# Retuning an instruction planner: longer v runs, a moved constant load, and a new order around the first expert's gather

## The chip, the cores and the metric

The kernel runs on one core of a Trainium2 chip. The core has five engines with an instruction queue of their own: PE (TensorE: matrix products and transposes), DVE (VectorE), ACT (ScalarE), POOL (GpSimd) and SP (SyncE, which here only issues DMA transfers). Each engine takes its instructions strictly in the order in which the program lists them, and semaphores make it wait for data of another engine or of a transfer. The metric is the device time of one execution in microseconds (us); less is better.

## The reference

Three stages follow each other. The first is attention with a mask by hash bucket: a query sees only the keys whose six hash bits are its own.

```python
q_bits = (np.einsum('bhsd,dk->bhsk', q, proj) > 0).astype(np.int64)   # B=2, H=8, S=768, D=64, 6 bits
k_bits = (np.einsum('bhsd,dk->bhsk', k, proj) > 0).astype(np.int64)
mask = q_bucket[:, :, :, None] == k_bucket[:, :, None, :]
scores = np.where(mask, scale * np.matmul(q, k.transpose(0, 1, 3, 2)), -1000000000.0)
attn = softmax(scores)
x = np.matmul(attn, v)                       # becomes 1536 tokens x 512
h = np.maximum(x @ w_in, 0.0)                # 512 -> 2048
x = (h * h @ w_out)                          # 2048 -> 512
```

The third is a layer of eight experts with 192 places each. All (token, expert) pairs are taken in falling order of their logit; a token goes to the first expert that still has a place.

```python
logits = x @ w_gate                          # 1536 x 8
for idx in np.argsort(-logits.flatten()):
    tok, e = (int(idx) // E, int(idx) % E)
    if assigned[tok] >= 0 or counts[e] >= 192:
        continue
    assigned[tok] = e
    counts[e] += 1
for e in range(8):
    out[assigned == e] = np.maximum(x[assigned == e] @ w1[e], 0.0) @ w2[e]   # 512 -> 1024 -> 512
```

## The kernel before, in words

**Planner.** The kernel does not issue instructions as its code is written. Each piece is given to a planner (`Sched`, `S.add`) with an engine, a planned duration, the pieces that it depends on, a priority and the buffers that it takes and gives back. The planner makes one list for each engine. The tables `PR`, `MP`, `EP`, `RP`, `FP` and the numbers `PREP`, `PREP1` and `DL` are priorities and planned costs; changing them changes the order of the lists and nothing that is computed. A dependency in the planner places a piece in its list. Only a use of the same data makes a semaphore in the program.

**Attention.** Eight pairs of heads are worked on, in 96 units of 128 queries by 768 keys. Per unit: four score products on PE (L578), the maximum on DVE (L594), the exponential on ACT (L597), the normalisation on POOL (L606), transposes on PE (L614), a split into two float parts on ACT and DVE (L622, L626), and two products with v on PE (L635, L636). Scores and mask are one product: under the 64 rows of q and k stand 64 rows of a one-hot code of the bucket.

**Preparation of the next pair.** It runs among the units of the pair before. SP loads q, k and v (L449, 384 KB each). PE transposes q and k (L453), ACT and DVE split them (L456, L462, L464), PE takes the bit products (L486) and the one-hot products (L492), ACT writes the one-hot codes (L497, L499) and splits v (L504, with L508 on POOL). SP copies the parts to the rows of the score operand within the on-chip memory (L259).

**Router and experts.** After the two dense layers, the router gathers logits and ranks; the comparisons on DVE (L1357) compare each token's values with all others, and PE counts the comparisons by products with ones (L1364, twelve for a comparison). The indices of the first expert's tokens come out at L1487 (`ix`); POOL then gathers these tokens' rows in two indirect transfers (L1662), PE transposes them (L1680, L1682), DVE and ACT copy the result (L1689, L1687), and the first expert product starts (L1718). The routing of the second expert needs the counts: it begins with L1400. Where PE would be idle here, it runs products on constants whose results nobody reads (`keep`, L1094). POOL's slot casts follow the routing.

Of the kernel before, what the change touches and what calls it, by code (L numbers as in the profile page):

```python
# [7 lines left out]
F32 = mybir.dt.float32  # L8
R = mybir.dt.float32r
# [225 lines left out]
PREP, PW, DL = -21, 0.8, 3.5  # L235
PREP1 = 3
LDP = (2, 0)
PR = {"S": 10.5, "mx": 907, "ex": 577.5, "dn": -268.5, "rec": -506.5, "nrm": 32, "tp": 16, "hi": -161, "lo": -447.5, "pv": 16, "oa": 45.5, "od": 261, "pe": -93, "pa": -360, "pd": -559.5}
# [14 lines left out]
def attention(nc, S, ps, mem, ident, q, k, v, proj, pat, xhi, xlo):  # L253
# [185 lines left out]
    def pair(pr, cm):  # L439
# [61 lines left out]
        def v_act(h):  # L501
            if h == 0:
                T["V", pr] = mem(S.unit(T["vi", pr], "V"), [6, 2, 2, 64], R)
            nc.scalar.activation(T["V", pr][:, :, h, h], T["raw", pr, "v"][:, :, h], AF.Copy)  # L504

        def v_pool(h):
            V = T["V", pr]
            nc.gpsimd.tensor_tensor(V[:, :, h, 1 - h], T["raw", pr, "v"][:, :, h], V[:, :, h, h].bitcast(F32), op=OP.subtract)  # L508
# [207 lines left out]
MP = {"ac": -331, "h1": 412, "h2": 438.5, "ch": -270, "cv": -245, "sp": -195.5, "lg": -262, "ev": -350, "lv": 292, "c0": 4704.5, "c1": 6115, "b0": 487.5, "b1": 3914}  # L716


def mlp(nc, S, ps, mem, ident, xhi, xlo, w_in, w_out, w_gate, wgt, x2d, L, att):
# [285 lines left out]
    return [ld[n] for n in range(12)], st, [i for f in range(16) for i in Wd[f]], []  # L1005


EP = {"fr": -157.5, "lr": -611, "row": 283.5, "col": -247, "cp": 1168.5, "ca": 992.5, "gp": 518}
# [7 lines left out]
RP = {"fr": 355, "se": -191, "oh": 241.5, "G": 263, "A": 634, "lr": -371, "pf": 48, "id": -515.5, "gp": 334, "sq": -73, "G1": 273.5, "A1": 207, "ei": -374, "up": -78}  # L1016
ACT_TILES = {12: (10, 11), 9: (8,), 6: ()}
KEEP = 60
# [18 lines left out]
class Router:  # L1037
# [9 lines left out]
    def __init__(self, tc, ctx, mem, ident, rc):  # L1047
# [5 lines left out]
        nc.sync.dma_start(k, rc)  # L1053
# [914 lines left out]
```

## Time and profile before

| what | us |
|---|---|
| time, median of three runs (lowest, highest) | 778.84 (776.38, 780.49) |
| the profiled execution: time | 779.57 |
| the profiled execution: span of its instructions | 777.8 |
| PE busy in the span | 756.5 (97%) |
| DVE, ACT, POOL busy | 528.3, 420.0, 388.0 |
| mean granted clock of PE, as a share of full speed | 0.987 |

The span goes from the first to the last instruction of the execution; the time has 1.77 us more around it. By the lines that run in it, attention takes the first 258 us, the two dense layers the time to 545, the early router that to 560, the routing of the first expert that to 575, and the experts the rest. An engine is busy while one of its instructions runs; waiting in its queue is not counted.

### The profile page before, as it was taken

Reading aid. Unit: us, or ns where it says so; the run is one execution under the profiler, and the core shown is the slowest. Engines: PE = TensorE matmul, PEld = TensorE weight load, DVE = VectorE, ACT = ScalarE, POOL = GpSimd, SP = SyncE. Lnnn points to the kernel's source line nnn. Section 1 sums busy time; section 2 is a strip of 40 time slices with the busy share of each in tenths; the row PEclk is TensorE's granted clock in tenths of the full one; section 3 lists DMA queues with packets and bytes.
Section 4 is the critical chain, followed back from the end, with each engine's and each line's share of the span. In section 5 each row is a group of like instructions: output and inputs, shape, how many; then the busy total and the mean of one; then the engine's idle time right before and its main releaser. Section 6 shows DMA issues by size and latency. Waiting matters only on the chain.

```text
span 777.8 us, 13945 instructions
## 1 busy us (share of the span) xinstructions
PE 756.5 (97%) x5018; PEld 667.5 (86%) x5018; DVE 528.3 (68%) x1118; ACT 420.0 (54%) x837; POOL 388.0 (50%) x397
## 2 busy tenths in 40 slices
PE   8989999999998999999999999999999999999996
PEld 6767988988887899899899899898679998888885
DVE  6879989999999876822861772245877768763342
ACT  7878999999998764622432343243432322333332
POOL 3667878778888785642562463226421220242111
PEclk9999999999999999999999999999789999999999
DMA  7967576585531133310330110011266366789200
GB/s 174 240 147 165 124 160 142 126 174 136 127 85 56 62 104 106 109 54 1 109 109 2 54 55 1 7 75 54 79 206 220 112 239 221 258 286 342 91 20 21
DMA packets 87973, 94.34 MB, mean 121 GB/s; under 512 B 41920, under 2 KB 66880, under 8 KB 87904
## 3 DMA queue, kind: packets, MB, share of 16 engines
q1 hardware_dynamic: 85856, 87.16, 39.5%
q0 software_dynamic: 2048, 6.29, 2.5%
q8 instruction: 40, 0.66, 0.3%
q14 instruction: 29, 0.24, 0.1%
HBM read 63.55 MB, written 6.29 MB: 90 GB/s over the span
## 4 chain that ended last, share of the span: by engine, by line
PE 72%; issue 9%; DVE 6%; DMA 4%; ACT 4%; POOL 3%; SPq 2%; ACTq 0%; POOLq 0%; DVEq 0%
PE psS L829 11%; PE psTP L802 9%; PE psm L802 9%; PE psS L1718 7%; PE psS L578 5%; PE psS L1759 3%; PE psTP L829 3%; PE psTP L614 3%; PE psO L829 3%; SPq L259 2%; DVE p L626 2%; DMA f<-in_v_dram 2%; DMA r<-r 1%; DVE f L594 1%; PE psTP L1364 1%
## 5 line engine op out<-in xcount | busy, mean ns | idle before, releaser
L606 POOL TENSOR_TENSOR f<-f 128x768 f32<-128x768 f32 x96 | 140.6, 1467 | 28.8 <-PE psTP L614 8.8
L815 POOL TENSOR_TENSOR r<-f,r 128x384 fp32r<-128x384 f32 x64 | 86.5, 1357 | 90.5 <-ACT r L813 77.9
L829 PE MATMUL psS<-r 128*128 128x512 f32 x384 | 95.9, 395 | 0.0
L594 DVE TENSOR_REDUCE f<-psS 128x1 f32<-128x768 f32 x96 | 90.9, 948 | 6.5 <-PE psS L578 6.3
L578 PE MATMUL psS<-r 128*128 128x384 f32 x384 | 88.0, 350 | 2.0 <-ACT f L597 1.1
L597 ACT ACTIVATE f<-psS,f 128x768 f32<-128x768 f32 x96 | 87.2, 909 | 4.3 <-DVE f L594 1.4
L829 PEld LDWEIGHTS psS<-r 128*128 128x128 f32 x384 | 70.8, 188 | 13.1
L811 DVE TENSOR_TENSOR f<-f,psTP 128x384 f32<-128x384 f32 x32 | 17.7, 553 | 88.6 <-ACT f L809 88.3
L1718 PE MATMUL psS<-ff,rf 128*128 128x192 f32 x400 | 76.5, 332 | 0.0
L802 PE MATMUL psTP<-r 128*128 128x384 f32 x384 | 73.4, 338 | 0.7 <-POOL r L792 0.7
L802 PE MATMUL psm<-r 128*128 128x384 f32 x384 | 71.8, 334 | 0.0
L578 PEld LDWEIGHTS psS<-r 128*128 128x128 f32 x384 | 65.2, 188 | 6.6 <-ACT f L597 4.8
L802 PEld LDWEIGHTS psTP<-r 128*128 128x128 f32 x384 | 67.9, 188 | 3.1 <-POOL r L792 1.0
L802 PEld LDWEIGHTS psm<-r 128*128 128x128 f32 x384 | 67.1, 188 | 0.1
L1718 PEld LDWEIGHTS psS<-ff,rf 128*128 128x128 f32 x400 | 64.6, 190 | 1.1
L1662 POOL DMA_INDIRECT ff<-x2d,ix x16 | 19.2, 1200 | 88.0 <-DVE ix L1487 53.5
L1841 POOL DMA_INDIRECT out_dram<-ff,ix x16 | 16.7, 1047 | 92.0 <-DVE ff L1852 67.5
L626 DVE TENSOR_TENSOR p<-psTP,p 128x384 fp32r<-128x384 f32 x102 | 54.8, 547 | 5.0 <-ACT p L622 4.5
L813 ACT ACTIVATE r<-f 128x384 fp32r<-128x384 f32 x64 | 33.5, 523 | 39.3 <-DVE f L811 39.3
L792 POOL TENSOR_TENSOR r<-f,r 128x1024 fp32r<-128x1024 f32 x16 | 40.4, 2525 | 28.5 <-ACT r L790 28.2
L622 ACT ACTIVATE p<-psTP 128x384 fp32r<-128x384 f32 x102 | 49.7, 502 | 6.7 <-PE psTP L614 5.5
L809 ACT ACTIVATE f<-psTP 128x384 f32<-128x384 f32 x32 | 15.6, 489 | 64.5 <-PE psTP L802 63.2
(398 smaller groups left out, 1745.4 us busy)
## 6 DMA issues: line engine op xcount, KB each, us to landing
rf<-in_moe_w_dram SPq DMA_DIRECT2D x60, 512.0 KB, 6.2
r<-r SPq DMA_DIRECT2D x90, 192.0 KB, 4.1
f<-in_moe_w_in_dram SPq DMA_DIRECT2D x16, 512.0 KB, 3.7
f<-in_moe_w_out_dram SPq DMA_DIRECT2D x16, 512.0 KB, 4.6
r<-r SPq DMA_DIRECT2D x15, 384.0 KB, 3.8
f<-in_q_dram SPq DMA_DIRECT2D x8, 384.0 KB, 5.2
f<-in_k_dram SPq DMA_DIRECT2D x8, 384.0 KB, 5.8
f<-in_v_dram SPq DMA_DIRECT2D x8, 384.0 KB, 4.7
```

Of the source, the lines that this page charges most:

```text
L578: nc.tensor.matmul(sbank(u)[:, hf, 0:384], T["q", (pr, h)][:, n, 128 * i:128 * i + 128], T["k", (pr, h)][:, n, 384 * hf:384 * hf + 384], s ...
L594: nc.vector.tensor_reduce(col(0, u), sbank(u)[:, :, 0:384], axis=AX.XY, op=OP.max, negate=True)
L597: nc.scalar.activation(P(u).rearrange("p (a b) -> p a b", a=2), sbank(u)[:, :, 0:384], AF.Exp, bias=col(0, u), accum_out=col(1, u))
L606: nc.gpsimd.tensor_tensor(Pn(u), P(u), col(3, u).to_broadcast([128, 768]), op=OP.mult)
L622: nc.scalar.activation(th, tp(u, g), AF.Copy)
L626: nc.vector.tensor_tensor(tl, tp(u, g), th.bitcast(F32), op=OP.subtract)
L792: nc.gpsimd.tensor_tensor(lo, F, hi.bitcast(F32), op=OP.subtract)
L802: nc.tensor.matmul(hbank(s, hf), w[:, c], y[:, x, sl], start=(c == 0 and i == 0), stop=(c == 3 and i == 2))
L813: nc.scalar.activation(hh[:, sl], r, AF.Copy)
L815: nc.gpsimd.tensor_tensor(hl[:, sl], r, hh[:, sl].bitcast(F32), op=OP.subtract)
L829: nc.tensor.matmul(abank(i), a[:, t], w, start=(f == RUNS[r][1][0] and j == 0), stop=(f == RUNS[r][1][-1] and j == 2))
L1718: nc.tensor.matmul(abank(n)[:, j], raw(p, g)[:, 0, 256 * c + 128 * j:256 * c + 128 * j + 128], xT(p)[:, c], start=(c == 0), stop=(c == 3))
```

## The change

It has four parts.

1. The load of v puts the two heads of a pair one after the other in a partition, so that a partition's piece of a head is one run of 1536 bytes in both memories instead of six of 256. The split of v (L504, L508) reads the new layout.
2. Planned costs of the transfers and of the first gather, and all priority tables, are replaced. This moves instructions on every engine.
3. The load of the router's constants (`rck`, L1053 in the kernel before, the first transfer on SP) is handed to the planner, which puts it eighth.
4. In the second phase of the first routing, the comparisons on DVE from the third on get a planner dependency on the first gather, and POOL's slot casts one on the last early comparison. The idle-time products of `keep` write a spare bank of the tile `z` (two of its banks belong to it, one was unused) instead of taking a bank from the pool; they may be placed from the end of the dense layers on, and 90 of them are allowed instead of 60.

```diff
-PREP, PW, DL = -21, 0.8, 3.5
-PREP1 = 3
+PREP, PW, DL = 56.5, 0.8, 2.4
+PREP1 = -29.5
...
-            a = T["raw", pr, nm] = mem(S.unit(T["li", pr, nm], "raw" + nm), [6, 2, 64])
-            nc.sync.dma_start(a, {"q": q, "k": k, "v": v}[nm][b, hh:hh + 2].rearrange("h (p j) d -> p j h d", p=128))
+            x = {"q": q, "k": k, "v": v}[nm][b, hh:hh + 2]
+            a = T["raw", pr, nm] = mem(S.unit(T["li", pr, nm], "raw" + nm), [2, 6, 64] if nm == "v" else [6, 2, 64])
+            if nm == "v":
+                nc.sync.dma_start(a.rearrange("p h j d -> p h (j d)"), x.rearrange("h (p j) d -> p h (j d)", p=128))
+            else:
+                nc.sync.dma_start(a, x.rearrange("h (p j) d -> p j h d", p=128))
...
-            nc.scalar.activation(T["V", pr][:, :, h, h], T["raw", pr, "v"][:, :, h], AF.Copy)
+            nc.scalar.activation(T["V", pr][:, :, h, h], T["raw", pr, "v"][:, h], AF.Copy)
...
-            ld[nm] = S.add("DMA", 2.1, None, [s], prio=base - 20, lat=1.8)
+            ld[nm] = S.add("DMA", 1.1 if nm == "v" else 1.75, None, [s], prio=base - 20, lat=1.9)
...
-            return S.add("DMA", 1.1 if nm == "oh" else 1.65, None, [s], prio=prio(x) - 40, lat=DL)
+            return S.add("DMA", 1.85 if nm == "oh" else 2.75, None, [s], prio=prio(x) - 40, lat=DL)
...
-        nc.sync.dma_start(k, rc)
...
+        z = self.st["z"]
+
         def f():
-            self.nc.tensor.matmul(ps(S.unit(a, "B")), self.ones, self.ones[:, None, :].to_broadcast([128, 4, 128]), start=True, stop=True)
-        a = S.add("PE", .215, f, [dep], prio=60, acq="B", half=1)
-        S.add("NONE", 0.0, None, [a, end], rel=[("B", a)])
+            self.nc.tensor.matmul(ps(S.unit(z, "S"))[:, 1], self.ones, self.ones[:, None, :].to_broadcast([128, 4, 128]), start=True, stop=True)
+        a = S.add("PE", .215, f, [dep, z], prio=60, half=1)
+        S.add("NONE", 0.0, None, [a, end, self.counted], rel=[("S", z)])
...
-                a = S.add("DVE", .13 + .00052 * W, lambda k=k: g_dve(k, 0), [*st["lrd"], war], prio=RP["G1" if ph == 1 else "G"])
+                a = S.add("DVE", .13 + .00052 * W, lambda k=k: g_dve(k, 0), [*st["lrd"], war, self.gather if ph == 1 and len(c) > 1 else None], prio=RP["G1" if ph == 1 else "G"])
...
-        T["ga", p] = ga = S.add("POOL", 2.1 if p else 3.6, gather, [ids], prio=FP["ga"], acq="xg")
+        T["ga", p] = ga = S.add("POOL", 2.1, gather, [ids], prio=FP["ga"], acq="xg")
+        if p == 0:
+            router.gather = ga
...
-    router.keep(S, ps, front, T["A", 0])
+    router.keep(S, ps, last, T["A", 0])
...
+        S.add("SP", .45, lambda: nc.sync.dma_start(router.k, rc), prio=-50)
...
-        experts(tc, nc, S, ps, mem, ident, router, x2d, w1, w2, out, L, cst, router.slots_(L)[-1])
+        experts(tc, nc, S, ps, mem, ident, router, x2d, w1, w2, out, L, cst, router.slots_([*L, *router.st["cmp"]])[-1], last)
```

Line numbers move by the edit: the loads are L451 (v) and L453 (q, k) in the changed kernel, and L453, L456, L486, L492, L497, L499, L504, L578, L597 and L622 become four more; L1357 becomes L1364, L1364 becomes L1371, L1400 becomes L1407, L1487 becomes L1496, L1689 becomes L1700.

**First place: SP, some 33 us into the run, where the second pair's v and the fourth pair's q and k are loaded** (the names behind the arrow are the sources; `r` is the memory of rounded operands, and the rows L259 are copies within it; the four `64x768` behind the loads copy the second pair's one-hot codes). Before:

```order
L259 DMA r_113<-r_113 64x768 x7
L449 DMA f_117<-in_v_dram 128x12x64
L449 DMA f_117<-in_q_dram 128x12x64
L449 DMA f_117<-in_k_dram 128x12x64
L259 DMA r_113<-r_113 64x768 x4
L259 DMA r_113<-r_113 64x2x768
```

And of the change:

```order
L259 DMA r_112<-r_112 64x768 x7
L453 DMA f_116<-in_q_dram 128x12x64
L453 DMA f_116<-in_k_dram 128x12x64
L259 DMA r_112<-r_112 64x768 x2
L451 DMA f_116<-in_v_dram 128x2x384
L259 DMA r_112<-r_112 64x768 x2
L259 DMA r_112<-r_112 64x2x768
```

The load of v went from ahead of q and k to behind both and behind two of the four copies of one-hot codes.

**Second place: ACT, some 40 us into the run, where the third pair's codes are made** (L597 is the exponential of a unit, L456 a part of q or k, L504 the split of the second pair's v, L644 an output, L497 and L499 the one-hot codes). Before, from the tenth unit's exponential on:

```order
L597 ACTIVATE f_117<-psS_71,f_117 128x768
L456 ACTIVATE r_113<-psTP_60 128x384
L504 ACTIVATE r_113<-f_117 128x6x64
L597 ACTIVATE f_117<-psS_67,f_117 128x768
L644 ACTIVATE f_117<-psm 64x384
L497 ACTIVATE r_113<-psTP_60,f_117 128x384
L499 ACTIVATE r_113<-psTP_61,f_117 128x384
L497 ACTIVATE r_113<-psO,f_117 128x384
L499 ACTIVATE r_113<-psTP_60,f_117 128x384
```

And of the change, from the eleventh exponential on, where the exponential is L601, a part of q or k L460, an output L648, and the codes L501 and L503:

```order
L601 ACTIVATE f_116<-psS_67,f_116 128x768
L460 ACTIVATE r_112<-psTP_61 128x384
L601 ACTIVATE f_116<-psS_71,f_116 128x768
L460 ACTIVATE r_112<-psTP_61 128x384
L501 ACTIVATE r_112<-psO,f_116 128x384
L648 ACTIVATE f_116<-psTP_60 64x384
L503 ACTIVATE r_112<-psTP_61,f_116 128x384
L501 ACTIVATE r_112<-psm,f_116 128x384
L503 ACTIVATE r_112<-psO,f_116 128x384
```

The split of v is gone from here (its two halves stand behind the fifteenth and sixteenth exponentials instead of the ninth and tenth), and the codes come one exponential later. On PE, the four one-hot products that these codes read stood behind the scores of eleven units (one) and twelve (three) and stand behind those of thirteen (two) and fourteen (two). In each later pair from the fifth on, on ACT, one code stood one exponential ahead of the other three, and all four now stand together where the three were.

**Third place: DVE, the routing of the first expert** (`ff` numbers are buffers, L1316 a sum of ranks, L1689 the copy of the transposed tokens). Before:

```order
L1357 TENSOR_SCALAR ff_5240<-ff_5238,mx 128x1536
L1487 CAST ix<-psTP_61 128x2
L1357 TENSOR_SCALAR ff_5241<-ff_5238,mx 128x1536
L1357 TENSOR_SCALAR ff_5242<-ff_5238,mx 128x1536
L1357 TENSOR_SCALAR ff_5239<-ff_5238,mx 128x1536
L1357 TENSOR_SCALAR ff_5240<-ff_5238,mx 128x1536
L1357 TENSOR_SCALAR ff_5241<-ff_5238,mx 128x1536
L1357 TENSOR_SCALAR ff_5242<-ff_5238,mx 128x1536
L1357 TENSOR_SCALAR ff_5239<-ff_5238,mx 128x1536
L1357 TENSOR_SCALAR ff_5240<-ff_5238,mx 128x1536
L1316 TENSOR_TENSOR PM<-PM,mx 128x96
L1689 COPY ff_5230<-psTP_61 128x384
```

And of the change, with the comparisons as L1364, the sum as L1323 and the copy as L1700:

```order
L1364 TENSOR_SCALAR ff_5245<-ff_5243,mx 128x1536
L1496 CAST ix<-psO 128x2
L1323 TENSOR_TENSOR PM<-PM,mx 128x96
L1364 TENSOR_SCALAR ff_5246<-ff_5243,mx 128x1536
L1364 TENSOR_SCALAR ff_5247<-ff_5243,mx 128x1536
L1364 TENSOR_SCALAR ff_5244<-ff_5243,mx 128x1536
L1364 TENSOR_SCALAR ff_5245<-ff_5243,mx 128x1536
L1364 TENSOR_SCALAR ff_5246<-ff_5243,mx 128x1536
L1700 COPY ff_5235<-psTP_61 128x384
L1364 TENSOR_SCALAR ff_5247<-ff_5243,mx 128x1536
L1364 TENSOR_SCALAR ff_5244<-ff_5243,mx 128x1536
L1364 TENSOR_SCALAR ff_5245<-ff_5243,mx 128x1536
```

Three comparisons went behind the copy of the transposed tokens, and five stand between `ix` and that copy instead of eight. On PE the transposes of the tokens (L1680 before) stood behind eleven of the second phase's twelve groups of counts and stand behind seven now; the other five groups are spread among the first products of the expert, with one, three, one, two and four of these between and behind them.

## Rows read from the trace of the kernel before

**Rows 1.** The page, busy time of each engine.

```profile
PE 756.5 (97%) x5018; PEld 667.5 (86%) x5018; DVE 528.3 (68%) x1118; ACT 420.0 (54%) x837; POOL 388.0 (50%) x397
```

**Rows 2.** Windows: length; busy us of PE, PEld, DVE, ACT, POOL; clock, DMA share, GB/s.

```profile
40.00:50.00 10.00, 7.15 (x43) 5.28 (x44) 6.52 (x14) 7.36 (x18) 5.25 (x8) 1.00 0.95 216
...
110.00:190.00 80.00, 79.71 (x525) 71.94 (x525) 75.13 (x157) 74.82 (x170) 64.09 (x73) 1.00 0.67 145
...
566.00:575.00 9.00, 8.79 (x135) 5.50 (x135) 7.02 (x9) 3.79 (x4) 4.35 (x3) 0.62 0.34 103
...
580.00:760.00 180.00, 180.00 (x1437) 161.84 (x1436) 111.48 (x358) 56.87 (x87) 34.07 (x50) 1.00 0.57 200
```

**Rows 3.** Timeline of the start: start us, us, instruction [idle before <-releaser].

```profile
0.73 0.40 SPq L1053 DMA_DIRECT2D rck<-in_rc_dram  x1
...
1.19 0.42 SPq L334 DMA_DIRECT2D f<-in_k_dram  x1
...
4.07 1.01 DVE L340 COPY f<-f 128x384 f32<-128x384 f32 x2 [3.18 <-DMA f<-in_k_dram]
```

**Rows 4.** Timeline, 27 to 50 us: loads, copies and waits.

```profile
28.45 0.76 PE L578 MATMUL psS<-r 128*128 128x384 f32 x3 [0.82 <-DMA r<-r]
...
32.98 0.89 SPq L449 DMA_DIRECT2D f<-in_v_dram  x1
...
35.34 3.26 SPq L449 DMA_DIRECT2D f<-in_k_dram  x1
...
38.70 11.35 SPq L259 DMA_DIRECT2D r<-r  x11
...
39.09 0.52 ACT L504 ACTIVATE r<-f 128x384 fp32r<-128x384 f32 x1 [1.66 <-DMA f<-in_v_dram]
```

**Rows 5.** The same timeline, 45 to 49 us.

```profile
45.74 0.58 ACT L497 ACTIVATE r<-psTP,f 128x384 fp32r<-128x384 f32 x1 [2.40 <-DMA r<-r]
...
46.38 0.32 PE L492 MATMUL psTP<-f 128*128 128x384 bf16 x1 [2.40 <-ACT r L497]
```

**Rows 6.** The page, DMA issues: number, KB each, us to landing.

```profile
r<-r SPq DMA_DIRECT2D x15, 384.0 KB, 3.8
...
f<-in_v_dram SPq DMA_DIRECT2D x8, 384.0 KB, 4.7
```

**Rows 7.** Timeline, 71 to 74 us.

```profile
71.87 0.52 ACT L504 ACTIVATE r<-f 128x384 fp32r<-128x384 f32 x1 [1.57 <-DMA f<-in_v_dram]
...
73.33 0.96 PE L578 MATMUL psS<-r 128*128 128x384 f32 x4 [0.41 <-ACT f L597]
```

**Rows 8.** Timeline of DVE, 562 to 578 us.

```profile
565.34 7.52 DVE L1357 TENSOR_SCALAR ff<-ff,mx 128x1536 bf16<-128x1536 f32 x8
...
575.03 0.56 DVE L1689 COPY ff<-psTP 128x384 f32<-128x384 f32 x1 [2.00 <-PE psTP L1680]
```

**Rows 9.** Timeline of POOL, 562 to 596 us: the first and the second gather.

```profile
566.37 1.98 POOL L1662 DMA_INDIRECT ff<-x2d,ix  x1 [12.93 <-ACT ff L1355]
568.66 1.51 POOL L1662 DMA_INDIRECT ff<-x2d,ix  x1 [0.30 <-issue]
...
587.84 1.44 POOL L1662 DMA_INDIRECT ff<-x2d,ix  x1 [16.81 <-DVE ix L1487]
589.59 0.92 POOL L1662 DMA_INDIRECT ff<-x2d,ix  x1 [0.30 <-issue]
```

**Rows 10.** DMA issues from 568.6 to 570 us: number, us to landing.

```profile
ff<-x2d,ix POOLq DMA_INDIRECT x1, 3.5
```

**Rows 11.** Timeline of PE, 571 to 577 us.

```profile
572.47 1.01 PE L1094 MATMUL psO<-ones 128*128 128x512 bf16 x2
573.28 0.51 PE L1364 MATMUL psTP<-Bb,ff 128*128 128x8 bf16 x12
573.64 0.58 PE L1680 MATMUL psm<-ident,ff 128*128 128x128 f32 x2
...
575.13 1.87 PE L1718 MATMUL psS<-ff,rf 128*128 128x192 f32 x10
```

More of the change, by code (lines that the diff above doesn't have):

```diff
@@ L715 @@
 LEAST = 3.4332275390625e-05
-MP = {"ac": -331, "h1": 412, "h2": 438.5, "ch": -270, "cv": -245, "sp": -195.5, "lg": -262, "ev": -350, "lv": 292, "c0": 4704.5, "c1": 6115, "b0": 487.5, "b1": 3914}
+MP = {"ac": -1376.5, "h1": 760, "h2": 1218, "ch": -2739, "cv": -1619.5, "sp": 462, "lg": 544.5, "ev": 332.5, "lv": 292, "c0": 6896, "c1": 5643.5, "b0": 632, "b1": 1725}
 def mlp(nc, S, ps, mem, ident, xhi, xlo, w_in, w_out, w_gate, wgt, x2d, L, att):
@@ L1004, in mlp @@
                 out(6 * b + n, z)
-    return [ld[n] for n in range(12)], st, [i for f in range(16) for i in Wd[f]], []
-EP = {"fr": -157.5, "lr": -611, "row": 283.5, "col": -247, "cp": 1168.5, "ca": 992.5, "gp": 518}
+    return [ld[n] for n in range(12)], st, [i for f in range(16) for i in Wd[f]], [], L2[NS - 1, ORD[-1]]
+EP = {"fr": -700, "lr": -268, "row": 2477.5, "col": 1099.5, "cp": 548, "ca": 768, "gp": 1400.5}
 CP = (5, 2, 4, 2, 1, 0)
@@ L1015 @@
 ND = 4
-RP = {"fr": 355, "se": -191, "oh": 241.5, "G": 263, "A": 634, "lr": -371, "pf": 48, "id": -515.5, "gp": 334, "sq": -73, "G1": 273.5, "A1": 207, "ei": -374, "up": -78}
+RP = {"fr": 1482.5, "se": -1108.5, "oh": -468, "G": 744.5, "A": 289, "lr": 155, "pf": 668, "id": 31, "gp": 453, "sq": 626, "G1": -523.5, "A1": -135.5, "ei": 1254, "up": 298.5}
 ACT_TILES = {12: (10, 11), 9: (8,), 6: ()}
-KEEP = 60
+KEEP = 90
 CW = .05
@@ L1170, in early @@
         left = [0]
-        st = {"lrp": None, "mx": None, "z": None, "g": []}
+        st = {"lrp": None, "mx": None, "z": None, "g": [], "cmp": []}
         E = {k: v + MB + 310 for k, v in EP.items()}
@@ L1251, in col @@
             if m:
-                part(range(m), [dve(.06 + .133 * m, f, deps, "col")])
+                d = dve(.06 + .133 * m, f, deps, "col")
+                st["cmp"].append(d)
+                part(range(m), [d])
             if np_:
@@ L1291, in early @@
             Bb = Bb1
-        self.st = {"g": st["g"], "z": T["z"], "Bb": Bb, "mx": m}
+        self.st = {"g": st["g"], "z": T["z"], "Bb": Bb, "mx": m, "cmp": st["cmp"][-1:]}
         return st["g"]
@@ L1401, in rest @@
         fu = dve(.09, cn, gl)
-        z1 = dve(d3, lambda: V.tensor_scalar(t("Z", [n, 8]), T["R"][:, 0:8 * n].rearrange("p (i e) -> p i e", e=8), 191.5, HUGE, op0=OP.is_gt, op1=OP.mult), [*gl, fu], rel=[(st["unit"], T["z"])])
+        z1 = dve(d3, lambda: V.tensor_scalar(t("Z", [n, 8]), T["R"][:, 0:8 * n].rearrange("p (i e) -> p i e", e=8), 191.5, HUGE, op0=OP.is_gt, op1=OP.mult), [*gl, fu], rel=[("B", T["z"])] if st["unit"] == "B" else ())
+        if ph == 0:
+            self.counted = z1
         z2 = dve(d3, lambda: V.tensor_tensor(T["Z"], T["Z"], T["PM"], op=OP.add), [z1, st["pm"]])
@@ L1591, in squeeze @@
         st["L"], st["alive"], st["tok"] = a, None, e1
-FP = {"ga": -188, "xp": -435.5, "xe": 7, "m1": 459.5, "re": -69.5, "m2": 30.5, "ye": -493.5, "yt": 339, "yo": -266, "sc": 92.5, "sp": -342.5, "mr": 123.5}
+FP = {"ga": -586, "xp": 1529.5, "xe": -755, "m1": 714, "re": -222, "m2": 315, "ye": -435, "yt": 641.5, "yo": -2360, "sc": 180.5, "sp": -1458.5, "mr": -908}
 AP = 5
@@ L1605, with experts @@
 MMR = .2285
-def experts(tc, nc, S, ps, mem, ident, router, x2d, w1, w2, out, L, cst, slot):
+def experts(tc, nc, S, ps, mem, ident, router, x2d, w1, w2, out, L, cst, slot, last):
     T = {}
@@ L1887, in experts @@
     next(phases)
-    front = router.st["mx"]
     before(0)
     add1(0, 0)
-    router.keep(S, ps, front, T["A", 0])
+    router.keep(S, ps, last, T["A", 0])
     for p in range(8):
@@ L1923, in whole @@
         S = Sched({**UNITS_A, **UNITS_M, **UNITS_F})
+        S.add("SP", .45, lambda: nc.sync.dma_start(router.k, rc), prio=-50)
         att = attention(nc, S, ps, mem, ident, q, k, v, proj, pat, xhi, xlo)
-        L, st, free, dots = mlp(nc, S, ps, mem, ident, xhi, xlo, w_in.bitcast(I32), w_out.bitcast(I32), w_gate, wgt, x2d, router.L, att)
+        L, st, free, dots, last = mlp(nc, S, ps, mem, ident, xhi, xlo, w_in.bitcast(I32), w_out.bitcast(I32), w_gate, wgt, x2d, router.L, att)
         cst = router.smalls(S, [i for e in att[0] for i in e])
```

4 lines of the change are left out of this document (2 added, 2 removed).

## Prediction

> **What bounds the kernel now.** I read the busy line first: PE is busy for 756.5 of 777.8 us and no other engine for more than 68% of it [rows 1]. So I looked for the stretches in which PE is not full, since only there can a new order give time back. By the windows, PE does 79.71 us in the 80 from 110 to 190 and all 180 from 580 to 760, but 7.15 of the 10 from 40 to 50 [rows 2]. From 566 to 575 it counts as busy with 8.79 of 9, at a granted clock of 0.62 of full speed [rows 2]; there the busy time is largely products that nobody reads, and the chain that decides is indices, gather, transposes, copy, first expert product. I then read the idle time ahead of single instructions in these stretches, to see what ended it:
> - The start: DVE is idle 3.18 us until k has landed; k's load is SP's second transfer, issued at 1.19, behind the constants at 0.73 [rows 3].
> - PE's scores wait 0.82 us for an on-chip copy at 28.45. At 46.38 PE waits 2.40 us for ACT, which had itself waited 2.40 us for copies [rows 4, 5].
> - ACT waits for v at 39.09 (1.66 us) and at 71.87 (1.57 us); the second of these lets PE wait 0.41 us for an exponential that stands behind the split [rows 4, 7].
> - The first gather's two instructions take 1.98 and 1.51 us on POOL, beside eight comparisons on DVE from 565.34 to 572.86; the transposes start at 573.64, the copy at 575.03, the first expert product at 575.13 [rows 8, 9, 11].
>
> All sums are made against the profiled execution's own 779.57 us (777.8 of span and 1.77 around it). It stands 0.73 us above the median of the runs, 778.84, so I take 0.73 off at the end.
>
> **The constants' load.** It is first on SP, and k's load is issued 1.19 - 0.73 = 0.46 us after it [rows 3]. Everything at the start hangs on k, so I count -0.5. Eighth in the queue it stands far ahead of the router, its first reader, 540 us later: the whole of attention covers it. Bounds: 0 (if another load ends the wait then) and -0.7.
>
> **The longer v runs.** The load's bytes stay, its runs grow from 256 to 1536 bytes. No row shows a load of 384 KB in such runs; the nearest is the on-chip copy of 384 KB in long rows, 3.8 us, against 4.7 for v now [rows 6]: some 0.9 us a load, eight loads. Only what ends a wait counts. The first v load shares the queue with the copy for which PE waits 0.82 us at 28.45; I take -0.6 of it, since the q and k loads ahead of that copy keep their short runs. Bounds 0 and -0.82. The wait at 71.87 was 1.57 us for v, which 0.9 shortens, and PE's part of it was 0.41: -0.4, bounds 0 and -0.41.
>
> The Trainium skill, page "DMA: Bandwidth & Descriptors", section "Specifications", says that pieces under 512 bytes don't reach the line rate, and its section "Anatomy of one DMA" gives 2.0 us and the bytes over 436 GB/s for one transfer, by which I estimate 2.9 us for a v load. By that page the gain is 1.8 us a load, and the first term would be the whole 0.82. The sum above goes by the row.
>
> **The new order around 33 to 50 us.** SP issued v, q and k, and k's issue took 3.26 us, until 38.60, before the second pair's one-hot codes could be copied from 38.70 on [rows 4]. The third pair's codes need the same buffers, so ACT waited for those copies until 45.74 and PE for ACT until 46.38 [rows 5]. Now two of these copies go ahead of v, whose issue took 0.89 us, and v's short runs no longer stand in the queue in front of k. I expect the two copies 2 to 3 us earlier and the other two 1.5 to 2.5. Beside it ACT's codes stand one unit later and PE has two units of transposes and v products in front of its last one-hot products, so that less must be hidden. Of the 2.40 us I take -2.0; bounds 0 (the queue of transfers is as full as before) and -2.4. The second pair's v is now some 5 us later, but its split stands five exponentials later on ACT; a unit takes 258/96 = 2.7 us (the attention stage by its 96 units), so some 13 us cover it.
>
> **The other attention tables.** PE is full in the steady stretch [rows 2], and in four pairs one code moves one exponential back. I count 0, bounds -1 and +3 (under the rivals).
>
> **The gather and the comparisons.** The new dependency stands in the planner alone. The comparisons and the gather share no data, so nothing in the program makes DVE wait for POOL; what changes is the list. Five comparisons follow the indices now, not eight: with 7.52/8 = 0.94 us each [rows 8] and the small sum ahead of them, DVE is free about 570.4. The gathers still run beside them, so I leave their times as they are: the second is issued at 568.66 and lands 3.5 us later, at 572.2 [rows 9, 10]. PE's transposes no longer stand behind the eleventh group of counts, which started at 573.28 [rows 11], only behind the seventh. So they start about 572.3, the copy follows about 573.6 instead of 575.03, and the first product at 573.8 instead of 575.13: a gain of up to 1.4.
>
> Then it is given back. The last three comparisons stand behind that copy on DVE and run from 574.1 to 574.1 + 3 x 0.94 = 576.9. PE's last groups of counts are placed between the first seven products and wait for them; the last group can start at 576.9 and ends at 577.4 (a group takes 0.51 us). By then PE has done seven products. Before, with 1.87/10 = 0.187 us a product [rows 11], the seventh ended at 575.13 + 1.31 = 576.44. PE is full from there to 760 [rows 2], so those 0.96 us stay, less a product or two of disorder: +0.8. Bounds -1.4 (if the products find no wait) and +1.5. The copy's POOL neighbours, the slot casts, wait for data as before: 0.
>
> What is late next is the second expert: its routing begins after the last count, some 2 us later than before. PE has 16 more products ahead of the second transposes than it had (56 instead of 40), 16 x 0.187 = 3.0 us, so I count 0; without that cover it would cost those 2 us.
>
> **The fillers.** They use a bank of their own and start earlier. One takes 1.01/2 = 0.5 us [rows 11]. One stands ahead of the reader of the counts, on the same tile, which can hold that reader by one filler: +0.2, bounds 0 and +0.5. If the clock were still 0.62 in the first ten products, they would take 1.87/0.62 - 1.87 = 1.1 us longer; I keep that as the upper bound of this term.
>
> **Sum.** -0.5 - 0.6 - 0.4 - 2.0 + 0 + 0.8 + 0.2 = -2.5 us, from 779.57 to 777.1, less 0.73: 776.3 us, 0.3% below the median. About 0.5%, 3.9 us, is what a measurement of this kernel can tell from no change, so this is the case "same", narrowly.
>
> **Rivals.**
> 1. *All waits go (faster).* With each attention term at its lower bound, -0.7 - 0.82 - 0.41 - 2.4, and the router at -1.4, the sum is -5.7: 773.1 us. For it: in attention every one of these waits ends on a transfer that the change touches. Against it: DVE's last comparisons stand behind the copy. Without the router's gain it is 775.3, within the bound; so it decides whether the counts hold PE. By the page's price for a v load the attention part lies at this end. Chance 0.33.
> 2. *The planner's wait works on the chip.* If the gather ran free of the comparisons, it would take what the second gather took, 1.44 + 0.92 instead of 1.98 + 1.51 [rows 9]: 1.1 us earlier, and 775.2 us. Against it: five comparisons still run beside it by the list. Chance 0.06.
> 3. *ACT's block of codes (slower).* Four codes of 0.58 us [rows 5] stand together in four pairs, and their copies may come late for the scores, which then wait. In the steady stretch ACT is busy 74.82 of 80 us [rows 2], so it has 6% of its time free, 0.17 us of a unit's 2.7. If a block lets PE wait 2.3 us (four codes), four pairs cost 9.3 us, and the time is 785.6. It decides from 1.6 us a pair on: 4 x 1.6 = 6.4 lifts 776.3 over 782.7. Against it: the last of the four codes stands where it stood. Chance 0.12.
>
> **The chances.** My own case has 0.47, the three rivals 0.33, 0.06 and 0.12, the rest 0.02. The first rival is spread around 773.1 and lies under 774.9 throughout; of my own case and the second some 0.06 lies there too. That gives faster 0.39, same 0.48, slower 0.13. The range goes from 770 (the first rival with three more microseconds from the steady stretch) to 781.5 (my case with its +3 there, +1.5 in the router and the filler's bound), which leaves out most of the third rival and little else.
>
> **What would show it.** k's first load issued near 0.75 and the span earlier by 0.5 us from there. The wait of 2.40 at 46.38 under 0.5. v loads near 3.8 us. Five comparisons behind the indices with no gap, three behind the copy, the transposes near 572.3, and PE's waits for DVE in the counts between the first products. PE at 80 of 80 in the steady stretch. The prediction is wrong if a new wait shows in attention where codes or copies are late, if the counts between the products don't hold PE, or if the second transposes wait.

## The result and the profile after

The changed kernel takes 785.37 us (median of eight runs, 782.61 to 786.13) against 778.88 for the kernel before in runs beside it. The ratio is 1.0071 with a 95% interval from 1.0053 to 1.0088: 0.7% slower. The prediction was 776.3, with 781.5 as its upper end. The profiled execution has a span of 783.5 us, 5.7 more than before.

I cut both spans at the same events, read from the records of single instructions:

| from | to | before | after | difference |
|---|---|---|---|---|
| start | last scores of attention | 257.16 | 255.76 | -1.4 |
| there | last second product of the dense layers | 289.07 | 292.39 | +3.3 |
| there | indices of the first expert | 19.04 | 18.82 | -0.2 |
| there | first expert product | 9.86 | 7.55 | -2.3 |
| there | end of the span | 202.67 | 208.97 | +6.3 |

So what I had costed (attention, and the stretch from the indices to the first product) did become shorter. The loss lies in the dense layers and behind the first expert product, stages in which PE was full before. Each row compares one profile with one profile. The last stretch took 209.0, 209.7 and 211.9 us in three profiles that have the changed kernel's list there, and 202.6, 202.7 and 206.5 in three that have the old one; how long the clock is halved in it differs from execution to execution.

The start and the loads, in the timeline of the changed kernel:

```profile
0.73 0.41 SPq L334 DMA_DIRECT2D f<-in_k_dram  x1
...
3.19 1.01 DVE L340 COPY f<-f 128x384 f32<-128x384 f32 x2 [2.31 <-DMA f<-in_k_dram]
...
27.90 0.76 PE L582 MATMUL psS<-r 128*128 128x384 f32 x3 [0.81 <-DMA r<-r]
...
32.74 1.18 SPq L453 DMA_DIRECT2D f<-in_k_dram  x1
...
34.01 4.59 SPq L259 DMA_DIRECT2D r<-r  x2
...
38.65 0.58 SPq L451 DMA_DIRECT2D f<-in_v_dram  x1
```

k is issued first, and DVE's wait fell from 3.18 to 2.31 us [rows 3]. The wait of PE at 28.45 [rows 4] is still there, at 27.90. k's second load now takes 1.18 us to issue instead of 3.26, and the copies start at 34.01, not at 38.70 [rows 4]; the waits of 2.40 us [rows 5] have no counterpart.

In the long stretch of attention there is a new wait, once in each of four pairs (timeline at the first of them):

```profile
104.91 0.58 ACT L503 ACTIVATE r<-psO,f 128x384 fp32r<-128x384 f32 x1
...
105.54 0.44 PE L639 MATMUL psO<-p,r 128*128 128x384 f32 x1 [0.53 <-ACT r L503]
```

A v product writes the bank `psO`, out of which ACT is still making a one-hot code. The same wait of 0.53 us stands at 136.18, 166.81 and 197.45.

In the dense layers PE waits for an addition on DVE that stands behind a conversion of weights (L788, 1.58 us):

```profile
375.51 1.58 DVE L788 SCALAR_TENSOR_TENSOR f<-f 128x1024 f32<-128x1024 f32 x1
...
377.01 1.27 DVE L850 TENSOR_TENSOR f<-psS,f 128x512 f32<-128x512 f32 x2
...
377.84 0.93 PE L833 MATMUL psS<-r 128*128 128x512 f32 x3 [0.90 <-DVE f L850]
```

It happens again at 445.42. The kernel before has only one wait above 0.2 us in this stage, at its start, and the changed one has that too.

The routing of the first expert, on DVE and POOL:

```profile
567.20 4.73 DVE L1364 TENSOR_SCALAR ff<-ff,mx 128x1536 bf16<-128x1536 f32 x5
574.40 0.56 DVE L1700 COPY ff<-psTP 128x384 f32<-128x384 f32 x1 [2.47 <-PE psTP L1691]
574.88 2.87 DVE L1364 TENSOR_SCALAR ff<-ff,mx 128x1536 bf16<-128x1536 f32 x3
```

```profile
568.07 1.22 POOL L1671 DMA_INDIRECT ff<-x2d,ix  x1 [11.37 <-issue]
569.60 1.51 POOL L1671 DMA_INDIRECT ff<-x2d,ix  x1 [0.30 <-issue]
```

Comparisons run beside both gathers, as the lists said. PE in the same stretch, first its timeline, then the windows of the profile (length; busy us of PE, PEld, DVE, ACT, POOL; granted clock, DMA share, GB/s):

```profile
571.37 0.76 PE L1371 MATMUL psTP<-Bb,ff 128*128 128x8 bf16 x24 [1.07 <-ACT ff L1362]
...
574.52 0.99 PE L1729 MATMUL psS<-ff,rf 128*128 128x192 f32 x2
575.30 0.51 PE L1371 MATMUL psTP<-Bb,ff 128*128 128x8 bf16 x12
575.67 2.27 PE L1729 MATMUL psS<-ff,rf 128*128 128x192 f32 x6
577.73 0.51 PE L1371 MATMUL psTP<-Bb,ff 128*128 128x8 bf16 x12
```

```profile
574.00:576.00 2.00, 2.00 (x29) 1.76 (x28) 1.60 (x3) 0.06 (x1) 0.00 (x0) 0.50 0.99 333
576.00:580.00 4.00, 4.00 (x34) 3.66 (x34) 1.75 (x2) 0.00 (x0) 0.00 (x0) 0.50 0.90 294
...
580.00:584.00 4.00, 4.00 (x35) 3.48 (x35) 1.66 (x9) 0.49 (x1) 0.00 (x0) 0.99 0.88 326
```

PE had stood idle for 0.45 us ahead of 568.25 and for 1.07 us ahead of 571.37. Then its clock is 0.50, the lower of its two levels (1.2 of 2.4 GHz), under the first products. Before, 0.62 from 566 to 575 was the mean of the stretch ahead of the products [rows 2], and the products ran at full clock:

```profile
574.00:576.00 2.00, 2.00 (x25) 1.77 (x24) 0.97 (x5) 0.49 (x1) 0.00 (x0) 1.00 0.92 249
576.00:580.00 4.00, 4.00 (x26) 3.55 (x25) 2.59 (x15) 0.49 (x1) 0.00 (x0) 1.00 1.04 367
```

Sixteen first products, with what stands between them, took 3.14 us before and take 6.57 now.

Behind that, the experts have two waits that the kernel before did not have, and one of 0.96 us near the end of it is gone:

```profile
622.87 0.38 PE L1371 MATMUL psTP<-Bb,ff 128*128 128x8 bf16 x9 [1.07 <-DVE ff L1364]
...
669.75 0.92 PE L1729 MATMUL psS<-ff,rf 128*128 128x192 f32 x4 [0.83 <-DVE ff L1700]
```

### The profile page after: what moved, and what is told of

It is laid out like the page before. It is cut to its first block, busy times and chain, and to the rows that moved or that the text cites. A ratio compares the mean times of both kernels' runs of the same rounds, so it can differ in the third digit from the quotient of the medians.

```text
span 783.5 us, 13939 instructions
## 1 busy us (share of the span) xinstructions
PE 760.6 (97%) x5017; PEld 670.4 (86%) x5017; DVE 522.8 (67%) x1118; ACT 422.6 (54%) x837; POOL 388.4 (50%) x397
## 4 chain that ended last, share of the span: by engine, by line
PE 75%; issue 10%; DVE 7%; ACT 3%; POOL 3%; DMA 2%; SPq 0%; POOLq 0%; DVEq 0%; ACTq 0%
PE psS L833 10%; PE psTP L806 8%; PE psS L582 7%; PE psO L806 7%; PE psS L1729 7%; PE psTP L618 4%; PE psm L833 3%; PE psTP L833 2%; PE psS L1770 2%; PE psm L618 2%; PE psO L639 2%; PE psTP L639 2%; PE psO L618 1%; PE psO L640 1%; PE psTP L640 1%
## 5 line engine op out<-in xcount | busy, mean ns | idle before, releaser
L819 POOL TENSOR_TENSOR r<-f,r 128x384 fp32r<-128x384 f32 x64 | 84.2, 1321 | 110.6 <-ACT r L817 93.0
L833 PE MATMUL psS<-r 128*128 128x512 f32 x384 | 100.8, 396 | 1.8 <-DVE f L850 1.8
L601 ACT ACTIVATE f<-psS,f 128x768 f32<-128x768 f32 x96 | 87.4, 910 | 5.7 <-POOL f L610 1.9
L1729 PE MATMUL psS<-ff,rf 128*128 128x192 f32 x400 | 80.0, 341 | 0.8 <-DVE ff L1700 0.8
L806 PE MATMUL psTP<-r 128*128 128x384 f32 x408 | 78.8, 339 | 0.7 <-POOL r L796 0.6
L806 PEld LDWEIGHTS psTP<-r 128*128 128x128 f32 x408 | 71.7, 188 | 3.9 <-POOL r L796 1.1
L806 PE MATMUL psO<-r 128*128 128x384 f32 x360 | 67.3, 334 | 0.0
L806 PEld LDWEIGHTS psO<-r 128*128 128x128 f32 x360 | 62.9, 188 | 0.1
L618 PE MATMUL psTP<-ident,f 128*128 128x128 f32 x312 | 50.4, 274 | 2.2 <-POOL f L610 1.0
```

Source lines behind the costliest of these rows:

```text
L601: nc.scalar.activation(P(u).rearrange("p (a b) -> p a b", a=2), sbank(u)[:, :, 0:384], AF.Exp, bias=col(0, u), accum_out=col(1, u))
L618: nc.tensor.transpose(tp(u, g)[:, j], Pn(u)[:, 128 * c:128 * c + 128], ident)
L806: nc.tensor.matmul(hbank(s, hf), w[:, c], y[:, x, sl], start=(c == 0 and i == 0), stop=(c == 3 and i == 2))
L819: nc.gpsimd.tensor_tensor(hl[:, sl], r, hh[:, sl].bitcast(F32), op=OP.subtract)
L833: nc.tensor.matmul(abank(i), a[:, t], w, start=(f == RUNS[r][1][0] and j == 0), stop=(f == RUNS[r][1][-1] and j == 2))
L1729: nc.tensor.matmul(abank(n)[:, j], raw(p, g)[:, 0, 256 * c + 128 * j:256 * c + 128 * j + 128], xT(p)[:, c], start=(c == 0), stop=(c == 3))
```

## The experiments

My theory after the result: the loss is three things behind attention, namely additions behind conversions in the dense layers, half clock under the first products, and new waits in the experts' order. The rival: attention's block of codes and the dense layers carry all of it, and the rest follows from their timing. Most of the edits below leave the lists of the other stages as they are; where they don't, it is said. Ratios are to the kernel before, run beside them on the same chip.

**The v runs alone.** The kernel before with the first part of the change alone (cut short here):

```diff
-            a = ... [6, 2, 64]
+            a = ... [2, 6, 64] if nm == "v" else [6, 2, 64]
-            ... T["raw", pr, "v"][:, :, h] ...
+            ... T["raw", pr, "v"][:, h] ...
```

> The kernel before with the longer v runs alone; its lists of instructions are those of before. If the waits for v and for the transfers queued behind it are what the runs shorten (0.82 us of PE at 28.45, 0.41 at 73.33, less than 0.9 a load elsewhere), 1.0 us comes off, 777.9 against 778.9. If v was hidden anyway, no change within 0.3 us. If the long runs do harm (larger bursts in front of the copies), 780 or more.

Measured: 0.9955 (0.9929 to 0.998), faster, and more than expected. On SP:

```profile
31.89 0.85 SPq L451 DMA_DIRECT2D f<-in_v_dram  x1
32.79 0.96 SPq L453 DMA_DIRECT2D f<-in_q_dram  x1
33.84 1.66 SPq L453 DMA_DIRECT2D f<-in_k_dram  x1
```

The load of v itself is not shorter: its median is 5.2 us here, 4.5 in the changed kernel, 4.7 before [rows 6]. What is shorter is the issue of the loads behind it: k's 1.66 us instead of 3.26 [rows 4] (1.13 to 1.74 in three other profiles with long runs on the old order, 2.32 in another with short ones). In its profile the wait of 0.41 us at 73.33 [rows 7] is gone, and 0.34 us are left of the 0.82 at 28.45 [rows 4]. The wait of 2.40 us for ACT [rows 5] is still there, with 2.10 us:

```profile
44.74 0.32 PE L496 MATMUL psTP<-f 128*128 128x384 bf16 x1 [2.10 <-ACT r L501]
```

Attention ends at 253.91 instead of 257.16; from its first scores to its last that is 242.6 us instead of 245.4. Its profile also has half clock from 614 to 621, which costs it 3.8 us in the experts; the kernel before, with the same lists, has none there.

**The old table in the dense layers.** The changed kernel with:

```diff
-MP = {"ac": -1376.5, ... "cv": -1619.5, ...}
+MP = {"ac": -331, ... "cv": -245, ...}
```

> The changed kernel with the priority table of the dense layers (MP) of before; the lists differ from the changed kernel's in the dense layers alone. My theory (the loss lies in three stages behind attention, the dense layers' part being two waits of 0.90 us at 377.84 and 445.42 and their surroundings): 3.3 us come off, 782.1. Rival (the early router absorbs what the dense layers lose): 785.4, no change against the changed kernel.

Measured: 0.998 (0.9957 to 1.0004). The dense layers end 3.5 us earlier (544.66), as expected. Part of the rest of the gain is behind them, where the lists differ too: the planner fitted 33 fillers into the router where the changed kernel has 28, and the first sixteen products took 4.24 us, not 6.57.

**Old router and experts.** The changed kernel with the tables `EP`, `RP`, `FP` and everything of the change's fourth part as before.

> The changed kernel with the router's and the experts' tables, the comparisons' dependency, the slot casts and the fillers of before; attention and dense layers have the changed kernel's lists. My theory: half clock at the first products (3.4 us) and waits in the experts (4 us) go, and the first product starts some 2.3 us later against the end of the dense layers; 778.9 - 1.4 (attention) + 3.3 (dense layers) = 780.8. Rival (attention's block of codes and the dense layers carry the loss): 784 or more.

Measured: 1.0092 (1.0055 to 1.0128). The expectation fell; the rival's number came, but not for its reason. From the first product to the end it takes 203.8 us, near the 202.67 of before, so most of those 6.3 us do belong to the new lists. But the new dense layers and the old early router don't fit: 96 of the router's counting products now stand ahead of the last second product, which comes at 553.11, and PE waits 1.74 us for POOL at 557.84. A stage's table can't be judged apart from its neighbour's.

**More fillers.** The changed kernel with two, four and two more products on constants:

```diff
+XG = {2: 2, 4: 4, 6: 2}
...
+        self.fill = f
...
+            for _ in range(XG.get(len(done), 0) if ph == 1 else 0):
+                self.fill()
             for i in range(n):
                 nc.tensor.matmul(Rv[:, i], G[:, 128 * i:128 * i + 128], T["Bb"][:, k], ...)
```

> The changed kernel with eight more products on constants among the last counts of the first routing (two, four and two ahead of the third, fifth and seventh group of counts), so that PE does not stand idle from 570.3 to 571.4. They compute nothing that is read. If the half clock from 573.4 to 580 comes of that idle time, the clock is full there and 3 us come off: 782.4. Rival (the counts' waits for the last three comparisons set the pace there, whatever the clock): 785 to 786.

Measured: 1.0026 (1.0003 to 1.0049), 0.45% less than the changed kernel, 3.5 us; the two intervals just don't meet. The windows of its profile:

```profile
574.00:576.00 2.00, 2.00 (x36) 1.90 (x33) 2.00 (x3) 0.00 (x0) 0.00 (x0) 1.00 1.02 360
576.00:580.00 4.00, 4.00 (x46) 3.48 (x42) 1.85 (x7) 0.49 (x1) 0.00 (x0) 1.00 0.99 328
```

The clock is full, and sixteen products take 4.24 us. So what PE does ahead of the first products decides their clock: eight more wide products keep it full, and the half clock costs 2.3 us there; the other 1.1 against 3.14 are the counts placed among the products. Whether the idle time lets the clock fall or the narrow counting products do is not shown; the last experiment bears on it. The stretch from the first product to the end is no shorter in this profile (209.24 us against 208.97), since its clock is halved from 618.9 and from 666.7 for 3.4 us each. The gain shows in the time of all runs, and in their mean granted clock: 0.989 over the twelve of this kernel, 0.986 over the changed kernel's eight. The kernel before has 0.985 to 0.988 on the chips of the experiments, so the changed kernel does not seem to be at half clock for longer than it; what differs is which products are under it.

**The constants' load.** The v runs, and the load of the constants eighth on SP by hand.

> The kernel before with the longer v runs and the constants' load eighth on SP by hand; all other lists as before. My theory: the moved load gives 0.5 to 0.9 us beside what the v runs give (3.5 us by ratio in the first experiment): a ratio near 0.994, some 4.2 us off. Rival (k's landing is not what the start hangs on): the first experiment's 0.9955.

Measured: 0.9958 (0.9932 to 0.9985), the rival's number. In its profile the first scores start at 10.97 instead of 11.78, but the start shifts by more than that among runs of the same loads (11.34 and 13.59 in two others with the constants first). Still, they start at 10.57 to 11.32 in all ten profiles with the load moved, and at 11.34 to 13.59 in all four with it first, so the start does come earlier. What that is worth in the time stays below what these runs can tell.

**Conversions behind additions.** One number of the changed kernel:

```diff
-"cv": -1619.5
+"cv": -1300
```

> The changed kernel with one number changed: the planner's priority of the weight conversions on DVE (cv) from -1619.5 to -1300, so that they stand behind the additions of the partial sums (ac, -1376.5), as they did before (-245 behind -331). Four instructions of DVE move, in the dense layers, none on other engines. My theory: the waits of 0.90 us at 377.84 and 445.42 go, 2.3 us come off, ratio to before 1.004. Rival (PE meets the same lateness somewhere behind): 1.007 as the changed kernel.

Measured: 1.004 (1.0015 to 1.0065), as expected, though this interval and the changed kernel's overlap. The stage itself is clearer: from the last scores of attention to the last second product it takes 290.15 us, not 292.39, so 2.2 us less, and 1.1 more than before. The timeline shows the conversion L788 behind the additions, and PE's products without a wait:

```profile
375.11 1.28 DVE L850 TENSOR_TENSOR f<-psS,f 128x512 f32<-128x512 f32 x2
...
376.31 0.69 DVE L850 TENSOR_TENSOR f<-psTP,f 128x512 f32<-128x512 f32 x1
376.38 0.84 PE L833 MATMUL psS<-r 128*128 128x512 f32 x3
...
378.10 1.22 DVE L788 SCALAR_TENSOR_TENSOR f<-f 128x1024 f32<-128x1024 f32 x1
```

**No fillers.** The kernel before with `KEEP = 0` in place of 60.

> The kernel before without the products on constants (the planner may place none instead of 60); attention and dense layers have the lists of before, the router's counts and a few rows behind move a little. Theory (what PE did before the first products decides their clock): half clock at the first products, 3 us slower, 782. Rival (the clock there comes of the products themselves, fillers or not): no change within 1 us.

Measured: 1.0036 (1.0012 to 1.0061), 2.8 us slower. The windows of its profile:

```profile
566.00:574.00 8.00, 4.97 (x133) 4.24 (x134) 8.00 (x10) 5.10 (x4) 4.35 (x3) 0.66 0.17 51
574.00:576.00 2.00, 2.00 (x23) 1.49 (x21) 0.59 (x2) 0.49 (x1) 0.00 (x0) 0.50 0.61 189
576.00:580.00 4.00, 4.00 (x16) 3.28 (x14) 2.67 (x14) 0.00 (x0) 0.00 (x0) 0.50 0.95 317
```

PE is idle for 3 of the 8 us ahead, and the first sixteen products take 5.97 us instead of 3.14: the same half clock, made in the kernel before.

**The new router on the kernel before.** The kernel as run kept the longer v runs as well, which its expectation leaves out.

> The kernel before with the changed kernel's router and experts alone (tables EP, RP, FP, the comparisons' dependency, the slot casts, the fillers' bank); attention, loads and dense layers as before. By the sum of stages of the changed kernel: first product 2.5 us earlier, half clock at the first products +3.4, two waits in the experts +1.9, the end +1.0, so 3.8 us slower, ratio 1.005. Rival (the half clock belongs to the new dense layers' timing): near 1.000.

Measured: 1.0037 (1.0011 to 1.0062). Against the v runs alone (0.9955) that is some 6 us more, the size of the stage behind the first product in the table above, and more than the 3.8 of the theory. Here too it isn't only the first products: with 45 fillers they run at full clock, and half clock comes from 620.8 to 627.6, beginning in a wait of PE for a comparison. The indices also come later, 21.3 us behind the dense layers instead of 19.04.

```profile
621.18 0.40 PE L1372 MATMUL psTP<-Bb,ff 128*128 128x8 bf16 x9 [1.60 <-DVE ff L1365]
```

**Old attention.** The changed kernel with `PR`, `PREP`, `PREP1`, `DL` and the planned transfer costs of before; v runs and constants' load as changed.

> The changed kernel with the attention tables and planned transfer costs of before (PR, PREP, PREP1, DL); v runs, constants' load, dense layers, router and experts as changed, and their lists equal the changed kernel's but for the number of products on constants. My theory: the four waits of 0.53 us of v products for ACT's codes go, and with them 1.8 us between the twenty-eighth and the last unit; 0 to 1.4 us come back ahead of that; ratio to before 1.005 to 1.007. Rival (the block of codes costs what I priced it at, 2.3 us a pair): 9 us off, ratio 0.996.

Measured: 1.0052 (1.0029 to 1.0075). The planner also fitted 45 fillers here instead of 28, and the first sixteen products run at full clock (4.23 us), so the ratio doesn't show attention alone. Its stretch does: the four waits of 0.53 us are gone. From the scores of the twenty-ninth unit to those of the ninety-third, PE takes 159.6 us, against 160.9 in the changed kernel and 158.5 to 159.5 in five profiles with the old lists. So the new tables cost 1.3 to 2.4 us there, not 9, which the four waits (2.1 us) can account for.

**No planner's wait.** The changed kernel without the dependency:

```diff
-[*st["lrd"], war, self.gather if ph == 1 and len(c) > 1 else None]
+[*st["lrd"], war]
```

> The changed kernel without the planner's dependency of the comparisons on the gather; attention and dense layers keep their lists, the routing's and the experts' change. If the dependency acts by the list alone, the two gathers take on POOL what they take in the changed kernel (1.22 and 1.51 us) to within 0.8 us, since comparisons run beside them in either. Rival (the dependency keeps the gather free): 2.7 us in the changed kernel's become 3.5 us or more here, and the first product comes 1 us or more later after the indices.

Measured: 1.0086 (1.0057 to 1.0114). The gathers' sum, 2.12 us, lies within the theory's bound, but not for its reason. Without the dependency the list puts the eight comparisons of the second phase that followed the indices ahead of them. The indices come at 573.94 instead of 566.97, and the gather runs alone:

```profile
575.15 1.20 POOL L1671 DMA_INDIRECT ff<-x2d,ix  x1 [18.90 <-PE psTP L1371]
576.66 0.92 POOL L1671 DMA_INDIRECT ff<-x2d,ix  x1 [0.30 <-issue]
```

So what the dependency does for the time is to keep comparisons behind the indices. That it works on the list alone is shown by the changed kernel's trace, where comparisons run beside both gathers. The second gather takes 0.92 us alone and 1.51 beside comparisons.

**Both cures.** The changed kernel with `cv` at -1300 and the eight more fillers.

> The changed kernel with both single cures together: the weight conversions behind the additions (four instructions of DVE) and the eight more products on constants. My theory: the two causes are separate stages and add up, 1.0071 - 0.0031 - 0.0045 = 0.9995, near the kernel before. Rival (one of them pays only where the other stands): 1.0026 to 1.004.

Measured: 0.9997 (0.9976 to 1.0018). The two causes are separate and add up, and together they are worth the whole net loss. They are not all that was lost: the dense layers keep 1.1 us (290.2), the stretch from the first product to the end takes 209.4 us in this profile, with half clock from 616.5 to 623.3, and shorter stages ahead of the first product go against that.

**Short runs in the changed kernel.** The load of v in runs of 256 bytes, everything else as changed.

> The changed kernel with the load of v in runs of 256 bytes as before; all lists are the changed kernel's. If the new order has taken v and its followers off the waits, the runs are worth under 1 us here: 1.007 to 1.009. Rival (the runs are worth here what they were worth on the lists of before, 3.5 us): 1.0115.

Measured: 1.0054 (1.0032 to 1.0075), no slower than with long runs (1.0071, the intervals overlap). On the new lists, where v stands behind q, k and two copies, the runs are worth nothing that can be measured.

The clock of this profile bears on what halves it. It falls at 567.8, behind 6.8 us in which PE is busy for 6.43 and waits only once for more than 0.15 us (0.22 at 567.00):

```profile
561.00:567.80 6.80, 6.43 (x107) 4.58 (x105) 6.67 (x22) 5.46 (x6) 0.72 (x1) 1.00 0.47 158
567.80:573.60 5.80, 5.54 (x75) 3.60 (x73) 3.25 (x5) 2.73 (x3) 2.86 (x3) 0.50 0.33 95
```

So the two waits of the changed kernel's profile, 0.45 and 1.07 us, are not needed for it. Its list between the indices and the first product has 8 fillers here as there, among narrow counts; the profiles with a full clock under the first products and the same list but for the fillers have 14 or 15.

The best of these is the kernel before with the longer v runs, 0.9955 with the constants' load left where it was, and 0.9958 with it moved: it beats both kernels.

## Why the prediction was wrong

**The failed step** is "only there can a new order give time back", of the stretches in which PE is not full. I wrote of attention's other tables "PE is full in the steady stretch", counted 0, and gave the dense layers' table no term at all, nor the experts' beyond the first products. But where PE is full, a new order can make it wait. The dense layers lost 3.3 us, of which one reversed pair of priorities (conversions ahead of additions) is 2.2 us by the stage and 0.31% by ratio, 2.4 us. The tables of the second experiment show this pair: `ac` -331 and `cv` -245 before, -1376.5 and -1619.5 now.

**The clock.** I kept half clock under the first products as an upper bound, +1.1, and took 0.2 for the fillers. It is there, and it costs 2.3 us in the first sixteen products and, by the experiment with more fillers, 0.45% by ratio. The step that failed is that the fillers "start earlier": I looked at which bank they use and not at where they end up. Between the indices and the first product there are 8 instead of 12, and PE waits there for some 1.7 us instead of 0.2. One of the waits that let it idle is for ACT's comparison at 571.37, on an engine whose list I had not read there.

**The counts among the products.** The +0.8 was the net of these counts and of the earlier first product, and at full clock the net is about nothing. The old list took 8.34 us from the indices to the first product and 3.14 for the first sixteen (profile of the constants' load), the new one 7.05 and 4.23 (profile with more fillers): 11.48 against 11.28. The counts cost 1.1 us and the earlier start gives them back. Between the two profiles of the result the net is +1.1, 13.00 against 14.12, with half clock ahead of the products in the one and under them in the other.

**From the indices to the first product** I expected 8.5 us and it took 7.55, since the first gather took 1.22 us instead of 1.98. It takes 1.20 to 1.22 us in all eight profiles in which it starts 0.9 us into a comparison, 1.96 to 1.98 in all five in which it starts 0.1 us into one, and 1.20 in the one in which it runs alone. The small sum that now stands ahead of the comparisons moved them by 0.17 us; I had left the gather's time as it was, and no experiment moves this alone. The 9.86 us of before hold 1.5 of half clock (8.34 in two profiles of the old list without it), so the list itself gains 1.2 to 1.3 us, near the 1.4 expected. Five comparisons, the copy, three comparisons: as the list said. That nothing on the chip makes DVE wait for POOL was right.

**Attention.** The start: -0.5 expected, 0.87 less of DVE's wait in the profile. The wait of 2.40 us: -2.0 expected, all of it gone, by the new order: it is 2.0 to 2.1 us in the four profiles with long runs on the old order, and not there with short runs on the new one. The wait at 71.87: gone. The wait of 0.82 us: -0.6 expected, nothing came off in the changed kernel. From its first scores to its last, attention is only 0.5 us shorter (244.9 against 245.4). The terms of the runs and of the order don't add up as I added them: it takes 244.2 to 244.9 us in all eight profiles with the new order, of which one has short runs, 242.6 to 244.4 in the four with the old order and long runs, and 245.4 and 246.1 in the two with the old order and short runs. Where the runs are long, the new order gains nothing here. The reason given for the term of 0.6 was wrong too: a v load takes 4.5 us and not 3.8. The Trainium skill's page "DMA: Bandwidth & Descriptors", section "Specifications", speaks of the line rate of pieces of 512 bytes and more; by the estimate from its section "Anatomy of one DMA", which is written for transfers issued from GpSimd, while SP issues these, a load would take 2.9 us. The measured 4.5 and 5.2 agree neither with this nor with my row; the loads shared the queues with q, k and the copies, and the long runs showed in how soon the next load could be issued.

**The slower rival** named the time, 785.6, by luck, for another reason. Its mechanism, a block of codes on ACT that makes PE wait in four pairs, is in the trace, with 0.53 us a pair where I wrote 2.3. These 2.1 us are a loss that attention's front part more than paid for.

**What stays open.** Of the 6.3 us behind the first product, 2.3 are the half clock, 1.1 the counts, and 0.9 the waits of 1.07 and 0.83 less the 0.96 that went. The other 2.0 lie under a busy PE, and no row holds them alone. This sum holds for the two profiles of the result: in three others the first products run at full clock, and the stretch still takes 208.2 to 209.4 us, with half clock further on. What the experts' list costs apart from the clock, and 1.1 of the 3.3 us in the dense layers, stay open.

## What to carry to other kernels

A retuned table moves work in every stage: read the lists of all of them, above all where the bounding engine is full: no wait is left there to win back, and a new order can make new ones. A pair of priorities that changes places is the first thing to look for in such a diff. Ahead of a stage that is bound by PE, look at what PE does in the microseconds before: eight products that nobody reads, put among narrow products and waits, gained 0.45% here. A single profile with one fall of the clock more or less can hide that, so read the time and the mean clock of all runs beside it. A transfer that is made cheaper may show its gain in the transfers issued behind it and not in its own time, and only on an order in which something waits for those. Two edits that shorten the same stretch, each alone, need not add up.

## What the runs showed of the hardware

The clock under the first products was half in all three profiles with the changed router's list as it is (16 products in 6.57, 6.65 and 6.15 us) and full in the five in which the planner or I put 33 to 45 fillers where the changed kernel has 28 (4.23 to 4.64 us). In attention it fell for 3.4 us, in or just behind PE's wait of 2.0 to 2.6 us for the codes, in four profiles of the old order (from 44.3, 46.4, 47.4 and 44.5), not in the two others of it, and in none of the eight with the new order, which have no such wait. Later in the experts it may fall or not with one and the same list: from 614 to 621 with the v runs alone, and not in the kernel before. Each such stretch takes back some 2 to 4 us, so that a single profile can hide a gain which the ratio over all runs shows.

An indirect gather on POOL ran beside comparisons on DVE, and its time followed from where in a comparison it started (1.20 to 1.22 us near the end of one, 1.96 to 1.98 near the start, 1.20 alone). An issue on SP took longer behind loads of short runs (k's 3.26 and 2.32 us on the old order) than behind one of long runs (1.13 to 1.74).
